# V loaded in three pieces between the pieces of w_in, the first FFN banks filled by head pairs, and a quarter of the first K loaded in float32 on another queue

## The chip, the cores and the metric

The kernel runs on one core of one Trainium2 chip. Times are device microseconds of that core. A "run" is one execution; a kernel's figure is the median of its runs. A profile is taken of one execution, and the spans and points in time in the text are that execution's. Engines: PE (TensorE matmul), PEld (its weight loads), DVE (VectorE), ACT (ScalarE), POOL (GpSimd), SP (SyncE).

## The reference

```
k_proj = einsum('ks,bhsd->bhkd', E, k)            # E, F: 64 x 1024
v_proj = einsum('ks,bhsd->bhkd', F, v)            # q, k, v: (8, 8, 1024, 64) float32
attn   = softmax(q @ k_proj^T / 8)
x      = (attn @ v_proj) as (8*1024, 512)
out    = relu(x @ w_in)^2 @ w_out                 # w_in 512 x 2048, w_out 2048 x 512
```

Eight batches, eight heads. Per batch the attention is small, and two FFN layers of 128x512 matmuls follow. The inputs are float32; the kernel computes in bfloat16 and lets GpSimd's DMA cast on the way in.

## The kernel before

The FFN of batch b runs on PE while the attention of the next batches is put between its steps. Only the first batch has nothing to hide behind: its loads, its attention and the weights come one after the other. The parts that matter here, with cuts marked:

```
    out_pool = ctx.enter_context(tc.tile_pool(name="outp", bufs=4))
    ...
    nc.sync.dma_start(e_f32[:], E[:])                      # SyncE's queue, no cast
    ...
    for g in range(2):                                     # GpSimd's queue, float32 -> bf16
        load(K0[:, half[g]], tokens(k, 0, h=half[g]))
        load(Q0[:, half[g], 0:4, :], tokens(q, 0, h=half[g], i=slice(0, 4)))
        ...                                                # F after the first Q
    for g in range(2):
        load(V0[:, half[g]], tokens(v, 0, h=half[g]))
    ...
    W_IN_PIECES = ((0, 2), (2, 4), (4, 8), (8, 12), (12, 16))
    ...                                                    # five pieces of w_in
    for j in range(WP):                                    # four pieces of w_out
        if j == WP - 1:
            load(Q0[:, :, 4:8, :], tokens(q, 0, i=slice(4, 8)))
        ...
    warm(8)                                                # matmuls on zeros
    ET = projection("ET", e_bf)
    ...                                                    # K, scores, V of both halves, values
    # FFN of the first batch, first layer: blocks fb = 0..15, four matmuls each over cb = 0..3;
    # then the second layer, w_out pieces 0..3 for two row tiles, step by step.
    # After step 21: transposes of the second half of Q.
```

A cb is a pair of heads: block fb can be begun with the pairs 0 and 1 only.

The softmax here doesn't subtract the row's maximum and nothing guards it: scores larger than these inputs give would overflow.

## Time and profile before

| | |
|---|---|
| median of 3 runs | 512.42 us (511.7 to 512.67) |
| profiled span | 510.0 us |
| PE busy | 497.0 us, 97% |
| first FFN matmul | 21.67 us |
| last w_out piece lands, PE goes on with it | 42.31, 42.35 us |

PE is full almost everywhere after 42 us. So a gain has to come from before. There the chain of waits (start, duration, what, in us) is a chain of loads:

```profile
7.67 14.18 DMA w_in_116<-in_moe_w_in_dram
21.86 0.28 issue
22.14 20.17 DMA w_out_131<-in_moe_w_out_dram
42.31 0.04 issue
42.35 1.04 PE ps_bank L364 x4
```

GpSimd issues the last piece of w_out (w_out_131) when the second piece of w_in has landed; it lands at 42.31, and PE uses it at once. PE's own timeline (start, duration, line, operation, tiles, shapes, count, and the idle time before it with its cause) shows the two places that the change aims at:

```profile
19.74 1.06 PE L204 MATMUL ps_bank<-V_sb,FT 128*64 128x256 bf16 x16 [1.44 <-DMA V_sb<-in_v_dram]
...
21.67 1.31 PE L358 MATMUL ps_bank<-xT,w_in_114 128*128 128x512 bf16 x5
...
25.57 3.62 PE L358 MATMUL ps_bank<-xT,w_in_118 128*128 128x512 bf16 x16
...
40.24 1.06 PE L231 MATMUL ps_bank<-ident,Q_sb 128*128 128x128 bf16 x16
...
42.35 1.02 PE L364 MATMUL ps_bank<-w_out_131,hsq 128*128 128x512 bf16 x4 [0.19 <-DMA w_out_131<-in_moe_w_out_dram]
```

PE is idle for 1.44 us before the second half of V, the FFN starts at 21.67, and its first four blocks are done when the next line starts, at 25.57. The windows view of the DMA engines in the first microseconds (window and length, then PE, PEld, DVE, ACT, POOL busy, then granted clock, DMA share, GB/s):

```profile
2.00:3.00 1.00, 1.00 (x4) 0.42 (x3) 0.00 (x0) 0.02 (x1) 1.00 (x3) 1.00 0.90 168
3.00:4.00 1.00, 1.00 (x4) 0.33 (x3) 0.00 (x0) 0.00 (x0) 0.95 (x4) 1.00 0.67 144
4.00:5.00 1.00, 0.79 (x2) 0.00 (x0) 0.64 (x1) 0.00 (x0) 1.00 (x2) 1.00 1.20 198
```

A share over 1 means that packets overlap. GB/s counts the bytes written: a cast load writes half of the float32 bytes that it reads. From 4 us to 42 us the share is about 1.2 to 1.4, with 180 to 205 GB/s written at first and 205 from 22 us on. Only the first two microseconds of transfer are not full.

### The profile page before, as it was taken

To read this page: it belongs to the slowest core of one execution; us is meant where nothing else is said; L and a number is where in the kernel's file an instruction comes from. 1 tells how busy PE (TensorE), PEld (TensorE's weight loads), DVE (VectorE), ACT (ScalarE), POOL (GpSimd) and SP (SyncE) were. 2 spreads that over 40 slices of the span, in tenths; PEclk is the share of its full clock that TensorE was granted. 3 is DMA by queue.
4 is the path that set the end of the run, shared out by engine and by line. 5 is a ranking of instruction groups with operands and counts; after the bars stand their busy time and mean duration, and the time that the engine had idled before them with its cause. 6 is when DMAs were issued, how large, how long until landed. Compare 5 with 4: busy or idle time off the path is not lost.

```text
span 510.0 us, 6889 instructions
## 1 busy us (share of the span) xinstructions
PE 497.0 (97%) x2710; PEld 222.8 (44%) x2761; DVE 216.7 (42%) x437; ACT 272.4 (53%) x411; POOL 32.0 (6%) x44
## 2 busy tenths in 40 slices
PE   8799999999999999999999999999999999999997
PEld 4344444444444444444444444444444444444444
DVE  2442766444434445235452345444443443522130
ACT  2564484664718556374645736366472755544351
POOL 7320100121000020001000000000000000000000
PEclk9999999999999999999999999999999999999999
DMA  9999999899996199104931060101102011010102
GB/s 156 204 205 222 226 207 202 132 220 207 195 217 125 56 185 201 65 0 126 181 78 42 17 160 1 62 22 42 53 1 82 1 41 42 31 54 21 63 0 82
DMA packets 67840, 53.92 MB, mean 106 GB/s; under 512 B 29152, under 2 KB 59616, under 8 KB 67808
## 3 DMA queue, kind: packets, MB, share of 16 engines
q0 software_dynamic: 30880, 29.49, 36.8%
q1 hardware_dynamic: 36928, 23.99, 17.5%
q8 instruction: 21, 0.34, 0.3%
q14 instruction: 11, 0.09, 0.1%
HBM read 59.24 MB, written 16.78 MB: 149 GB/s over the span
## 4 chain that ended last, share of the span: by engine, by line
PE 88%; DMA 7%; issue 2%; POOL 1%; ACT 1%; DVE 1%; POOLq 0%; ACTq 0%
PE ps_bank L364 41%; PE ps_bank L358 40%; DMA w_out_131<-in_moe_w_out_dram 4%; DMA w_in_116<-in_moe_w_in_dram 3%; PE ps_bank L185 2%; PE ps_att L256 1%; PE ps_att L290 1%; PE ps_att L312 1%; PE ps_bank L312 1%; DVE rs L300 0%; PE ps_bank L241 0%; DVE xT L341 0%; POOL K_sb L76 0%; POOL V_sb L76 0%; ACT expT L270 0%
## 5 line engine op out<-in xcount | busy, mean ns | idle before, releaser
L355 DVE TENSOR_TENSOR hsq<-h_relu 128x512 bf16<-128x512 bf16 x256 | 108.9, 426 | 192.9 <-ACT h_relu L354 192.0
L354 ACT ACTIVATE h_relu<-ps_bank 128x512 bf16<-128x512 f32 x256 | 151.7, 599 | 69.3 <-PE ps_bank L358 69.2
L364 PEld LDWEIGHTS <-hsq 128*128 128x128 bf16 x1040 | 99.5, 98 | 123.6 <-issue 9.3
L371 ACT COPY o_sb<-ps_bank 128x512 f32<-128x512 f32 (+1 forms) x65 | 37.6, 579 | 119.7 <-PE ps_bank L364 110.9
L364 PE MATMUL ps_bank<-w_out_124,hsq 128*128 128x512 bf16 (+1 forms) x257 | 65.6, 376 | 0.2
L364 PE MATMUL ps_bank<-w_out_131,hsq 128*128 128x512 bf16 (+1 forms) x251 | 64.1, 376 | 1.4 <-issue 1.1
L364 PE MATMUL ps_bank<-w_out_128,hsq 128*128 128x512 bf16 (+1 forms) x252 | 64.3, 376 | 1.1 <-issue 1.0
L364 PE MATMUL ps_bank<-w_out_126,hsq 128*128 128x512 bf16 (+1 forms) x249 | 64.2, 376 | 1.1 <-issue 0.8
L300 DVE COPY rs<-rs 32x1024 f32<-32x1024 f32 x60 | 41.3, 689 | 47.2 <-ACT rs L295 45.8
L358 PE MATMUL ps_bank<-xT,w_in_122 128*128 128x512 bf16 x255 | 58.9, 380 | 0.0
L358 PE MATMUL ps_bank<-xT,w_in_118 128*128 128x512 bf16 x250 | 57.7, 380 | 0.4
L358 PE MATMUL ps_bank<-xT,w_in_120 128*128 128x512 bf16 x247 | 57.4, 379 | 0.4
L270 ACT ACTIVATE expT<-ps_att 128x1024 bf16<-128x1024 f32 x32 | 31.8, 1024 | 18.1 <-PE ps_att L256 18.1
L358 PEld LDWEIGHTS <-w_in_120 128*128 128x128 bf16 x256 | 24.9, 98 | 30.4 <-issue 0.4
L358 PEld LDWEIGHTS <-w_in_118 128*128 128x128 bf16 x256 | 24.9, 98 | 30.2 <-issue 0.4
L358 PEld LDWEIGHTS <-w_in_122 128*128 128x128 bf16 x256 | 24.4, 98 | 31.1 <-issue 2.7
L358 PE MATMUL ps_bank<-xT,w_in_114 128*128 128x512 bf16 x128 | 30.6, 379 | 0.3 <-DVE xT L341 0.2
L358 PE MATMUL ps_bank<-xT,w_in_116 128*128 128x512 bf16 x126 | 30.0, 379 | 0.1
L294 ACT ACTIVATE rs<-ps_att 128x1024 f32<-128x1024 f32 x15 | 15.3, 1023 | 12.7 <-PE ps_att L290 12.7
L316 DVE TENSOR_TENSOR xT<-ps_att,rs 128x512 bf16<-128x512 f32 x28 | 18.1, 686 | 8.7 <-PE ps_att L312 8.4
L358 PEld LDWEIGHTS <-w_in_114 128*128 128x128 bf16 x128 | 12.4, 98 | 15.6 <-issue 1.3
L358 PEld LDWEIGHTS <-w_in_116 128*128 128x128 bf16 x128 | 12.5, 98 | 15.2 <-issue 0.2
(71 smaller groups left out, 233.9 us busy)
## 6 DMA issues: line engine op xcount, KB each, us to landing
out_dram<-o_sb SPq DMA_DIRECT2D x63, 256.0 KB, 2.0
K_sb<-in_k_dram POOLq DMA_DIRECT2D x7, 1024.0 KB, 22.1
V_sb<-in_v_dram POOLq DMA_DIRECT2D x7, 1024.0 KB, 26.7
Q_sb<-in_q_dram POOLq DMA_DIRECT2D x7, 1024.0 KB, 15.0
K_sb<-in_k_dram POOLq DMA_DIRECT2D x2, 512.0 KB, 7.1
V_sb<-in_v_dram POOLq DMA_DIRECT2D x2, 512.0 KB, 12.0
Q_sb<-in_q_dram POOLq DMA_DIRECT2D x2, 256.0 KB, 7.6
w_in_118<-in_moe_w_in_dram POOLq DMA_DIRECT2D x1, 512.0 KB, 15.5
```

The lines of the kernel that those rows point to most:

```text
L185: nc.tensor.matmul(ps[LO, :], lhsT=ET[:, i, :], rhs=self.K[:, :, i, :], start=f, stop=l)
L256: nc.tensor.matmul(ps[o, par], lhsT=self.kT[r, h % 4, h // 4, :], rhs=self.qT[r, h, n, :], start=True, stop=True)
L270: nc.scalar.activation(e[:], ps[:], AF.Exp, scale=SCALE)
L294: nc.scalar.activation(rs[1][:], ps[:], AF.Ln)
L300: nc.vector.tensor_copy(rs[j][lack:lack + 32], rs[j][have:have + 32])
L312: nc.tensor.matmul(ps_x[par][o], lhsT=self.vp[r, 2 * pr + a, :], rhs=e[r, par], start=True, stop=True)
L316: nc.vector.tensor_tensor(out=self.xT[:, pr, :, par], in0=ps_x[par].rearrange("p (c t) -> p c t", c=2), in1=rs[:, par].rearrange("p (c t) ...
L354: nc.scalar.activation(r[:], ps[:], AF.Relu)
L355: nc.vector.tensor_tensor(out=self.hsq[c][:, fb, :], in0=r[:], in1=r[:], op=ALU.mult)
L358: nc.tensor.matmul(ps[:], lhsT=w_in_blk(cb, fb), rhs=self.xT[:, cb, c].rearrange("p a t -> p (a t)"), start=(cb == 0), stop=(cb == NCB - 1),)
L364: nc.tensor.matmul(ps[:, m], lhsT=self.hsq[c][:, fb, tb * P:(tb + 1) * P], rhs=w_out_blk(fb)[:, m], start=(fb == 0), stop=(fb == NFB - 1),)
L371: nc.scalar.copy(o[:, m], ps[:, m])
```

## The change

Its intent: start the FFN before all of V is there, and load two heads of the first K without a cast, by a queue that starts earlier. The diff, cut:

```
+    k_f32 = soft_pool.tile([P, 2, NI, D], F32, tag="rs", name="k_f32")
+    nc.sync.dma_start(k_f32[:], tokens(k, 0, h=slice(0, 2)))
...
     for g in range(2):
-        load(K0[:, half[g]], tokens(k, 0, h=half[g]))
+        h = slice(2 if g == 0 else 4, 4 * g + 4)
+        load(K0[:, h], tokens(k, 0, h=h))
...
-    for g in range(2):
-        load(V0[:, half[g]], tokens(v, 0, h=half[g]))
+    V_PIECES = (slice(0, 4), slice(4, 6), slice(6, 8))
+    load(V0[:, V_PIECES[0]], tokens(v, 0, h=V_PIECES[0]))
...
     for j, (lo, hi) in enumerate(W_IN_PIECES):
         ...                                     # the piece of w_in
+        if j < 2:
+            load(V0[:, V_PIECES[j + 1]], tokens(v, 0, h=V_PIECES[j + 1]))
...
-                    banks = [bank() for _ in range(2)]
-                    for g in range(2):
-                        for fb in range(2):
-                            for cb in (2 * g, 2 * g + 1):
+                    banks = [bank() for _ in range(4)]
+                    for cbs, fbs in (
+                        ((0, 1), (0, 1)), ((0, 1), (2, 3)), ((2,), (0, 1)), ((2,), (2, 3)), ((3,), (0, 1, 2, 3)),
+                    ):
+                        for fb in fbs:
+                            for cb in cbs:
                                 self.first_mm(c, fb, cb, banks[fb])
...
+        nc.scalar.copy(K0[:, 0:2], k_f32[:])
...
-        att.project_v(1)
-        att.chunk_values(0, 1)
...
+                at(1, att.project_v, V_PIECES[1])
+                at(2, att.chunk_values, 0, 1, (0,))
+                at(2, att.project_v, V_PIECES[2])
+                at(3, att.chunk_values, 0, 1, (1,))
```

More of the change, by code (lines that the diff above doesn't have):

```diff
@@ L111 @@
     w_in_at, w_out_sb = {}, []
-    for lo, hi in W_IN_PIECES:
+    for j, (lo, hi) in enumerate(W_IN_PIECES):
         t = wpool.tile([P, NCB, (hi - lo) * P], BF16, name=f"w_in_{lo}")
@@ L197, in project_k, with project_v @@
             self.keep_k(ps[LO, 0:C // 2], g, nc.scalar.copy if g == 0 else None)
-        def project_v(self, g):
-            ps = bank()
+        def project_v(self, h):
+            n = (h.stop - h.start) * D
+            ps = att_psum()[:, 0, 0:n]
             for i in range(NI):
@@ L204, in project_v @@
                     nc.tensor.matmul(
-                        ps[o, 0:C // 2], lhsT=FT[:, i, :], rhs=V0[:, half[g], i, :],
-                        start=(i == 0), stop=(i == NI - 1),
+                        ps[o], lhsT=FT[:, i, :], rhs=V0[:, h, i, :], start=(i == 0), stop=(i == NI - 1)
                     )
-            nc.vector.tensor_copy(self.vp[:, half[g]], ps[:, 0:C // 2].rearrange("k (h d) -> k h d", d=D))
+            nc.vector.tensor_copy(self.vp[:, h], ps.rearrange("k (h d) -> k h d", d=D))
         def transpose_k(self, gs=(0, 1)):
@@ L331, in chunk_sums, with chunk_values @@
             self.rs[g] = self.inverse(ps)
-        def chunk_values(self, c, g):
+        def chunk_values(self, c, g, pairs=(0, 1)):
             ps = att_psum()
-            e, rs = self.e.pop(g), self.rs.pop(g)
-            for j in range(2):
+            e, rs = self.e[g], self.rs[g]
+            for j in pairs:
                 s = slice(j * HC, (j + 1) * HC)
                 self.values_mm(ps[:, :, s], 2 * g + j, e[:, :, s])
-            for j in range(2):
+            for j in pairs:
                 s = slice(j * HC, (j + 1) * HC)
@@ L380, in steps @@
                 if first:
-                    banks = [bank() for _ in range(2)]
-                    for g in range(2):
-                        for fb in range(2):
-                            for cb in (2 * g, 2 * g + 1):
+                    banks = [bank() for _ in range(4)]
[4 more added lines that the diff above has]
+                            for cb in cbs:
                                 self.first_mm(c, fb, cb, banks[fb])
-                            if g == 1:
+                            if cbs[-1] == NCB - 1:
                                 self.square(c, fb, banks[fb])
-                        yield
-                    fb0 = 2
+                        if (cbs, fbs) != ((2,), (2, 3)):
+                            yield
+                    fb0 = 4
                 for fb in range(fb0, NFB):
@@ L448 @@
         warm(2)
-        att.project_v(0)
+        att.project_v(V_PIECES[0])
         warm(1)
@@ L452 @@
         att.chunk_values(0, 0)
-        warm(1)
-        att.project_v(1)
-        att.chunk_values(0, 1)
+        warm(2)
         coming = None
```

## The prediction

> **What bounds the kernel now.** PE is busy 97% of the 510.0 us span (page, part 1) at a granted clock of 1.0, and the windows view shows it at 99% or so from 42.35 us on. The gain left lies before that. There PE works 17.06 of the first 21.67 us (with warm-up matmuls) and 20.17 of the next 20.68. In the chain of waits that stretch is DMA: w_in_116 (second w_in piece) lands at 21.86, GpSimd then issues the last w_out piece, which lands at 42.31, and PE, having waited only 0.19 us, goes on at 42.35. So PE and the load stream arrive together at 42.3 us. The DMA engines never rest before that: 205 GB/s (written bytes) in 21.67:42.35, one 512 KB piece per about 2.55 us, in order of issue.
>
> **What the change does.**
> 1. FFN start. Now the first FFN matmul waits for the second half of V (landed 19.7) and runs at 21.67. After the change w_in's first piece comes straight behind V's first half (16.0), so the first four FFN matmuls can run about 18.5 to 19.5. The price: V projection in 32 small matmuls among the FFN (about 1.3 us; L204's 16 of 256 columns take 1.06), and waits for V's last piece (about 21 to 21.5) and for two more rounds of copy, values, multiply. I expect the first four FFN blocks finished about 24.3 instead of 25.6: PE gains 1 to 1.5 us on the old order.
> 2. That alone gives nothing at 42.3: the bytes ahead of the last w_out piece are the same, so PE would just wait there about 1 us.
> 3. K in float32. 256 KB leave GpSimd's cast stream (1.28 us at 205 GB/s) and become 512 KB on SyncE's queue. The Trainium skill ("DMA: Bandwidth & Descriptors", section "Issuing engines are not separate DMA queues") says that all queues run on the same 16 engines, so this is no free bandwidth; in this trace the casts read about 410 GB/s of float32 and lone stores move 330 GB/s, so the 512 KB cost an estimated 1.3 to 1.55 us of the engines. What is won is that it fills the start: the first E packet runs at 2.1, the first cast packet at 3.2, and the engines are about half used from 2.5 to 4.0 (windows view: DMA share 0.90 and 0.67 against 1.2 to 1.4 later), an estimated 0.7 us of lost transfer time. Net: the cast stream, the last w_out piece too, lands about 0.6 us earlier (0.2 to 1.0). ScalarE's cast (about 1.0 us, as L270 of that size) fits before the ET copy ends at 6.37 and costs nothing.
>
> **On the critical path:** only the shift of the stream, about 0.6 us; after 42 us everything moves by it.
>
> **Prediction: 511.6 us, 80% range 510.4 to 512.6; faster by over 2% 0.01, within 2% 0.98, slower 0.01.**
>
> **What would show the steps.** Right: first FFN matmul before 19.5; the fourth FFN block done about 1.3 us earlier; last w_out piece landing at 41.3 to 42.1, and PE waiting 0.5 us or more for it (now 0.19); DMA share above 1 in 2:4. Wrong: w_out landing at 42.3 or later (the float32 load only pushes the casts back); PE idle over 2 us between 19 and 24.
>
> **What would make it wrong:** float32 loads that share the engines worse than estimated; E delayed by K; the new order of GpSimd's loads starving the stream; or something else in the stream relaxing, for 1.5 us or more.

## The result, and the profile after

The changed kernel took 512.45 us (median of 6 runs, 511.94 to 513.01), beside 512.54 us for before in the same rounds and its earlier runs. The ratio is 0.9993, with a 95% interval of 0.9975 to 1.001: the same. A ratio is the mean time of one kernel's runs over that of the other's of the same rounds, so not quite the ratio of the medians. The predicted 511.6 us lies 0.85 below; the range holds the result.

The chain of waits after:

```profile
8.37 13.37 DMA V_sb<-in_v_dram
21.74 0.28 issue
22.02 20.25 DMA w_out_134<-in_moe_w_out_dram
42.27 0.04 issue
42.31 1.04 PE ps_bank L370 x4
```

It is the same chain with other names, and it ends 0.04 us earlier, not 0.6. PE's timeline:

```profile
18.51 0.38 PE L364 MATMUL ps_bank<-xT,w_in_115 128*128 128x512 bf16 x1 [0.34 <-DVE xT L347]
...
21.78 0.64 PE L211 MATMUL ps_att<-V_sb,FT 128*64 128x128 bf16 x16
22.66 0.59 PE L364 MATMUL ps_bank<-xT,w_in_115 128*128 128x512 bf16 x2 [0.24 <-DVE xT L347]
...
24.28 0.59 PE L364 MATMUL ps_bank<-xT,w_in_115 128*128 128x512 bf16 x2 [0.26 <-DVE xT L347]
...
25.34 3.61 PE L364 MATMUL ps_bank<-xT,w_in_121 128*128 128x512 bf16 x16
...
42.31 1.02 PE L370 MATMUL ps_bank<-w_out_134,hsq 128*128 128x512 bf16 x4 [0.37 <-DMA w_out_134<-in_moe_w_out_dram]
```

The FFN starts 3.2 us earlier (18.51), but its first four blocks are done at 25.34, only 0.23 us before the old order. The last piece of V lands at 21.74, and from there the work goes through projection, copy, values and multiply, with PE waiting on DVE twice more (0.24 and 0.26 us). What PE gained, it then spends waiting for w_out. The windows view of the first transfers:

```profile
2.00:3.00 1.00, 1.00 (x4) 0.41 (x3) 0.00 (x0) 0.03 (x1) 1.00 (x4) 1.00 0.87 164
3.00:4.00 1.00, 1.00 (x4) 0.32 (x3) 0.00 (x0) 0.00 (x0) 0.93 (x4) 1.00 1.04 279
4.00:5.00 1.00, 0.79 (x2) 0.00 (x0) 0.60 (x1) 0.00 (x0) 1.00 (x2) 1.00 1.06 369
```

The float32 load fills 3 to 4 us (share 1.04 instead of 0.67), but it does nothing for 2 to 3 us. From 4 to 5 us, 369 GB/s instead of 198 is no gain: 198 GB/s of casts written are about 396 read. The first packet of GpSimd's casts runs at 4.84 us, where it ran at 3.22 before (from the packets of the trace). By 8 us the stream was about 0.4 us ahead all the same (by the packets, and counting the two heads of K as the 256 KB that they are in bfloat16, 874 KB against 791, at 205 GB/s). Then it slowed down: from 8 to 9 us the windows view shows 135 GB/s, where before has 196, and by 10 us about 0.15 us of the lead was left. Why it slowed down there is open.

One more thing. The profiled span of after is 1.2 us longer than before's, although its lead at 42 us is 0.04. I lined the two traces up at ScalarE's 65 copies of output tiles. After leads by 0.04 us from the first copy to the fourteenth (144 us) and is 1.34 us behind from the sixteenth (155 us) to the end. So the whole of it was lost between 144 and 155 us. The waits in 140:158 us (engine and line, what it waited for, us, times, longest), before:

```profile
ACT o_sb L371 <- DMA out_dram<-o_sb: 7.5, 2, 5.5
```

and after:

```profile
ACT o_sb L377 <- DMA out_dram<-o_sb: 8.9, 2, 7.7
...
PE ps_bank L364 <- ACT o_sb L377: 1.1, 2, 0.8
```

ScalarE's copy waits for an output buffer, because four stores are stuck on SyncE's queue: a DMA transpose of Q was issued there at 116.09 and holds the queue until 138.61, and the first store behind it was issued at 138.71 and landed at 152.26 (before: 137.38 and 150.13). In before the wait ends just in time, and its view has no line in which PE waits for the copy; here PE has to wait for its bank.

### The profile page after: what moved, and what is told of

Its sections match the earlier page's. It is cut to its first block, busy times and chain, and to the rows that moved or that the text cites. A ratio compares the mean times of both kernels' runs of the same rounds, so it can differ in the third digit from the quotient of the medians.

```text
span 511.2 us, 6930 instructions
## 1 busy us (share of the span) xinstructions
PE 498.3 (97%) x2727; PEld 223.3 (44%) x2778; DVE 217.0 (42%) x438; ACT 273.2 (53%) x412; POOL 33.0 (6%) x45
## 4 chain that ended last, share of the span: by engine, by line
PE 85%; DMA 9%; issue 2%; ACT 2%; POOL 1%; DVE 1%; SPq 0%; POOLq 0%; ACTq 0%
PE ps_bank L364 40%; PE ps_bank L370 38%; DMA w_out_134<-in_moe_w_out_dram 4%; DMA V_sb<-in_v_dram 3%; PE ps_bank L191 2%; DMA out_dram<-o_sb 2%; PE ps_att L262 1%; PE ps_att L296 1%; PE ps_att L318 1%; PE ps_bank L318 1%; DVE rs L306 1%; ACT rs L301 0%; ACT rs L300 0%; PE ps_bank L247 0%; ACT expT L276 0%
```

## The experiments

Theories: **G** (gate): PE and the load stream meet at the last w_out piece; its landing decides. Rival **P**: PE's order in the first blocks decides. **S** against **N**: the late stores take away, or do not take away, what the start gains. Later **C**: PE's clock at the start matters for the new order.

For every trace I read three times. "Landed" is when the last w_out piece has landed. "PE ready" is when PE could have started on that piece: its weight load for that matmul plus 0.21 us, the distance of the two where nothing held the matmul back. "Lag" is the end of the first and of the seventeenth output copy against before's (43.99 and 171.01 us); the difference of the two lags is what was lost in between, mostly at the late stores. "Full clock from" is the start of the trace's first record of the full granted clock.

| run | full clock from | PE ready | landed | lag, copy 1 | lag, copy 17 |
|---|---|---|---|---|---|
| before | 5.3 | 41.99 | 42.31 | 0 | 0 |
| after | 5.6 | 41.77 | 42.27 | -0.04 | 1.34 |
| e1_again | 4.2 | 41.57 | 41.73 | -0.57 | 0.26 |
| e2_no_f32 | 4.6 | 41.84 | 42.51 | 0.21 | 0.41 |
| e3_f32_only | 9.7 | 41.59 | 41.93 | -0.37 | 1.29 |
| e4_v_two | 9.5 | 42.51 | 41.95 | 0.18 | 0.12 |
| e5_before_b8 | 4.7 | 41.51 | 42.02 | -0.29 | -0.35 |
| e6_after_b8 | 9.3 | 42.96 | 41.87 | 0.62 | 0.56 |
| e7_v_two_b8 | 9.4 | 42.34 | 42.28 | 0.01 | -0.05 |
| e8_q_late | 4.1, half rate again 7.5 to 10.9 | 41.85 | 39.64 | -0.48 | 0.70 |
| e9_after_b8_warm | 4.7 | 41.53 | 42.07 | -0.23 | -0.29 |
| e10_before_b8_cold | 12.6 | 43.00 | 42.64 | 0.66 | 0.60 |
| e11_after_b8_cold | 10.5 | 43.31 | 42.09 | 0.97 | 0.91 |
| e12_q_late_warm | 4.3 | 40.50 | 39.29 | -1.84 | -0.65 |

(Copy 1 of e8 and e12 stands elsewhere in the order of work, so only their copy 17 compares. Their "PE ready" does not compare either: 16 transposes of Q, about 0.9 us of PE, stand before the last w_out piece in the other kernels and behind it in these two.) All twelve kernels gave the correct result. Four kernels at a time shared a chip and the runs of before.

### e1_again: the changed kernel once more

No edit.

> The changed kernel, unchanged, for a second trace and a tighter ratio. Theory G (gate): PE meets the load stream at the last w_out piece, so that piece's landing decides the time; it landed at 42.27 against 42.31 before, so the ratio is 0.999 to 1.001 and the landing again within 0.15 us of 42.3. Theory N (noise): the 1.38 us that the profiled run lost at 144 to 155 us, behind a late DMA transpose on SyncE's queue and late stores, is chance and comes in some runs of both kernels; then this trace shows another loss there, anything from 0 to 1.5 us. If it belongs to the change, it is there again with 1.1 to 1.5 us of PE idle.

Measured: 512.4 us, ratio 0.9996 (0.998 to 1.0012), before 512.68. The ratio is as theory G has it, but the landing is not: 41.73 us, 0.58 before the old one and 0.54 before the same kernel's first trace. So the stream varies by half a microsecond between runs of one kernel, and this trace shows the shift that I had predicted. The loss at the late stores was there again, but 0.83 us instead of 1.38. Expected for chance was anything from 0 to 1.5; it is neither absent nor of one size, so this trace alone does not tell chance from the change (see e5 and e6).

### e2_no_f32: without the float32 K

```
-    k_f32 = ...; nc.sync.dma_start(k_f32[:], ...)
-        h = slice(2 if g == 0 else 4, 4 * g + 4)
+        h = half[g]
-        nc.scalar.copy(K0[:, 0:2], k_f32[:])
```

> The change without the float32 K: V in three pieces and the FFN by head pairs stay. Theory G: first FFN matmul near 18.9 (0.35 later than after), last w_out piece lands at 42.5 to 42.6 (before's 42.31 plus about 0.2 for the extra piece), time 0.1 to 0.3 us over before, ratio 1.000 to 1.001. Rival P (PE's early start is worth something by itself): time 0.2 us or more below before although the stream is not earlier.

Measured: 512.34 us, ratio 0.9998 (0.9984 to 1.0011). First FFN matmul at 18.69, landing at 42.51, as theory G had it; PE was ready 0.67 us before. Theory G holds in the trace: the FFN starts 3 us earlier, and the first output copy ends 0.21 us later than before.

### e3_f32_only: before, with only the float32 K

```
+    k_f32 = ...; nc.sync.dma_start(k_f32[:], tokens(k, 0, h=slice(0, 2)))
+        h = slice(2 if g == 0 else 4, 4 * g + 4)
+        load(K0[:, h], tokens(k, 0, h=h))
+        nc.scalar.copy(K0[:, 0:2], k_f32[:])
```

> Before, with two heads of K in float32 through SyncE's queue and nothing else. Theory G with the stream earlier by 0.35 us (what the loads of K and Q showed in after): last w_out piece lands at 41.9 to 42.1, PE arrives for it at the same time as before or 0.3 earlier, span 0.2 to 0.35 us below before, ratio 0.9993 to 0.9996. My prediction's term (0.6 us won at the start): landing at 41.6 to 41.8. First cast packet at 4.8, not 3.2, in either case.

Measured: 512.04 us, ratio 0.9989 (0.9973 to 1.0005). Landing at 41.93, first output copy 0.37 us earlier: with the float32 K alone the stream is 0.38 us earlier than in before, and PE follows it. One trace does not show that the float32 K made this shift: e5, the old order without it, landed at 42.02. It then lost 1.66 us at the late stores, so its profiled span was 511.2. One expectation failed: the first cast packet ran at 3.54, not 4.8 (4.20 in e1_again). The casts do not simply queue behind the float32 load; how the engines share the two queues differs from run to run.

This trace also showed something that I had not looked for: PE ran at half rate from 5.9 to 9.7 us (see e6), and yet PE was ready at 41.59. In the old order the wait for V hides a slow start.

### e4_v_two: V's second half in one piece

```
-    V_PIECES = (slice(0, 4), slice(4, 6), slice(6, 8))
+    V_PIECES = (slice(0, 4), slice(4, 8))
-        if j < 2:
+        if j < 1:
-                at(2, att.chunk_values, 0, 1, (0,))
-                at(2, att.project_v, V_PIECES[2])
-                at(3, att.chunk_values, 0, 1, (1,))
+                at(1, att.chunk_values, 0, 1)
```

> After, with V's second half in one piece behind w_in's first piece, so the chain from V to the last xT is one round of copy, values and multiply instead of two. PE should finish the first four FFN blocks at 24.0 to 24.5 instead of 25.3. Theory G: that buys nothing, PE waits 1.0 us or more for the last w_out piece (0.37 in after), which lands at 42.1 to 42.3, and the time is that of after within 0.2 us. Rival P: the time falls by 0.8 us or more with the earlier blocks.

Measured: 511.9 us, ratio 0.9988 (0.9975 to 1.0002), 0.5 us in the median below e1_again of the same rounds, between what G and P expected. The trace cannot tell them apart, because PE started slowly in it (half rate up to 9.5 us), the blocks were done about 26 us, and PE came after the landing. So PE was not waiting for the stream here at all, and the 0.5 us are inside the noise of the runs.

### e5_before_b8 and e6_after_b8: the late stores taken away

Both with this edit, nothing else; a copy then finds a free buffer while four stores wait:

```
-    out_pool = ctx.enter_context(tc.tile_pool(name="outp", bufs=4))
+    out_pool = ctx.enter_context(tc.tile_pool(name="outp", bufs=8))
```

> Before with eight output buffers instead of four, to take away the wait that ScalarE's output copy has near 145 to 152 us for a store that stands behind a DMA transpose on SyncE's queue. Theory S (the late stores take away what the start gains, and are the spread of the runs): no PE idle at 144 to 156 us, runs spread by less than 1 us (before: 511.5 to 514.3), median 0.3 to 1.0 us below before. Rival N (the spread comes from elsewhere, the start or the launch): spread and median as before.

> After with eight output buffers. Theory S: PE loses nothing at 144 to 156 us, and what is left against the same change of before is the lead at the last w_out piece alone: 0.05 to 0.6 us below e5_before_b8, ratio to before 0.997 to 0.999. Rival N: the median stays within 0.2 us of after's 512.4.

Measured: e5 511.63 us (511.36 to 512.54), e6 511.97 us (511.07 to 512.4), before in the same rounds 512.42 (511.44 to 515.23). Both ratios are 0.9981 (0.9954 to 1.0007 and 0.9957 to 1.0006). In both traces the lag no longer changes between copies 1 and 17, within 0.06 us: the loss is gone, as theory S has it. The six runs each of e5 and e6 spread by 1.2 and 1.3 us, the eleven of before by 3.8. The gain of the median is inside the intervals, so S is shown in the traces and only likely in the times. Two expectations failed: e5's spread was to be under 1 us, and e6 was to be 0.05 to 0.6 us below e5, but its median is 0.34 above.

The record speaks against the late stores being the change's doing. The first store behind the transpose lands at any time from 150.13 to 152.37 us in the fourteen traces, and in the old order too (151.50 in e5, 151.73 in e10); before's 150.13 is the earliest of all. In the six traces with four buffers the loss grows with this landing, taken less the trace's own lag at copy 1: 150.13 in before and 150.46 in e4, with no loss; 151.17, 151.79, 152.30 and 152.74 in e2, e1, after and e3, with 0.20, 0.83, 1.38 and 1.66 us. So before's trace was a lucky one, and much of after's extra 1.2 us of span comes from comparing with it. A lead at the start makes the copies come sooner, and these stores do not follow.

With the stores out of the way the change is still worth nothing: 0.9981 against 0.9981. And e6's trace is 0.62 us behind before at copy 1, although its stream landed at 41.87. The reason is at the start. PE's timeline of after:

```profile
5.82 1.04 PE L151 MATMUL ps_bank<-zeros 128*128 128x512 bf16 x4
6.84 1.03 PE L200 MATMUL ps_bank<-K_sb,ET 128*64 128x256 bf16 x8
```

and of e6:

```profile
5.90 1.89 PE L151 MATMUL ps_bank<-zeros 128*128 128x512 bf16 x4
7.72 1.82 PE L200 MATMUL ps_bank<-K_sb,ET 128*64 128x256 bf16 x8
```

The same matmuls take 1.89 and 1.82 us instead of 1.04 and 1.03: half rate, until 9.3 us. The windows view prints a granted clock of 1.00 for these stretches too; durations tell it. The Trainium skill ("TensorE: Matmul & The Clock Gate", section "What's actually happening") says that the clock doubles after a busy window of about 3.4 us, and that this window is free-running, so that the moment varies from run to run. The traces agree: in e7, PE does the same as in after up to 5.8 us, and gets the full clock at 9.4 instead of 5.6; and in e8 the clock records change at 4.12, 7.53 and 10.95 us, 3.4 us apart.

For the old order such a start is free (e3: PE ready at 41.59). For the new order it is not (e6: 42.96, 1.2 us later than after's 41.77), because the idle 1.44 us before the second half of V, in which it could be made up, is what the change has removed.

### e7_v_two_b8: V in two pieces, eight buffers

The edits of e4 and e5 together.

> V's second half in one piece, with eight output buffers. Theory G (the landing of the last w_out piece decides): PE has the first four FFN blocks done at 24.0 to 24.6 when PE's clock is full at the start, waits 0.7 to 1.5 us for the last w_out piece at about 42, and the time is that of e6_after_b8 within 0.2 us. Rival P (PE's order decides): 0.6 us or more below e6_after_b8.

Measured: 511.46 us (511.21 to 512.05), ratio 0.9974 (0.995 to 0.9998), 0.5 us below e6 in the median, as e4 was below e1. The premise failed again: PE started slowly, so it was ready at 42.34 and met the landing at 42.28. Against e6, also slow at the start, it was ready 0.6 us sooner. So in these two traces the order with one round of copy, values and multiply does count when PE comes late, as rival P says; the difference of the times is inside the noise. I cannot tell how many of the timed runs start slowly, since they have no trace.

### e8_q_late: the gate moved

```
-        if j == WP - 1:
-            load(Q0[:, :, 4:8, :], tokens(q, 0, i=slice(4, 8)))
+    load(Q0[:, :, 4:8, :], tokens(q, 0, i=slice(4, 8)))       # after the last w_out piece
-                at(21, ...transpose_q_chunk x2)  at(23, ...chunk_scores x2)  at(25, att.sums, 0)
-                at(27, ...chunk_values x2)
+                at(25, ...transpose_q_chunk x2)  at(26, ...chunk_scores x2)
+                at(28, att.chunk_sums, 1, 0)  at(29, att.chunk_sums, 1, 1)
+                at(31, att.chunk_values, 1, 0)  at(32, att.chunk_values, 1, 1)
-                if first:                                     # banks by head pairs
+                if self.cold:                                 # ... in the second chunk as well
```

> e7 with the gate moved: the second half of Q is loaded after the last w_out piece, 512 KB less ahead of it, so that it lands at 39.3 to 39.8 instead of 42; the attention of the second chunk starts three steps later, with one sum per head group, and its FFN is filled by head pairs too. Theory G: now the early FFN start counts; the first output copy comes 1.0 to 1.6 us earlier than in e7, and the time is 0.7 to 1.5 us below e7's, if the later chunk does not stall PE by more than 0.5 us at 50 to 53 us. Rival P: no gain over e7, or a loss.

Measured: 511.0 us (510.73 to 512.31), ratio 0.9971 (0.9945 to 0.9996). The piece landed at 39.64, as expected, and PE passed it without a wait. But the profiled run (512.31, its slowest) was again one with half rate at the start, from 7.5 to 10.9 us, so PE was the late one: it began the piece 0.5 us before the old order did, but with about 0.9 us of transposes still to do, and was 0.70 behind at copy 17. The median is 0.46 below e7's, by the ratios only 0.15 us: less than theory G wanted, and no proof against P.

### e9_after_b8_warm, e10_before_b8_cold, e11_after_b8_cold: PE's clock at the start

```
-        warm(8)
+        warm(10)          # e9;  e10 and e11: warm(2)
```

e9 and e11 are e6 with that edit, e10 is e5 with it.

> After with eight output buffers and ten instead of eight warm-up matmuls at the start, which fill PE's idle 0.4 to 0.6 us before the transposes of E. Theory C (PE's clock at the start is a matter of chance in the runs: half rate up to 9.3 to 9.7 us in five of the seven float32 runs, full from 4.2 to 5.6 in the others; full rate is worth something to the new order): full rate from 7.5 us or sooner, the projection of K in about 1.05 us and not 1.9, last FFN block of the first four begun before 24.5, median 0.2 to 0.6 us below e6_after_b8. Rival N (the clock at the start is hidden behind the loads): half rate or not, the median is that of e6_after_b8 within 0.15 us.

> Before with eight output buffers and two warm-up matmuls instead of eight, so PE runs at half rate until about 9 us or later in every run. Theory C: the wait for V's second half (1.28 to 1.44 us of PE idle) hides most of it: median 0 to 0.4 us over e5_before_b8. Rival: it is in the time in full, 1.4 us over e5_before_b8.

> After with eight output buffers and two warm-up matmuls instead of eight. Theory C: the new order has used up the idle time in which before hides a slow start, so PE comes late to the last w_out piece, the first FFN matmul is at 19.8 or later, and the median is 0.8 to 1.5 us over e9_after_b8_warm, and 0.4 to 1.2 over e10_before_b8_cold. Rival N: within 0.2 us of e9_after_b8_warm and of e10_before_b8_cold.

Measured: e9 511.56 us (511.18 to 512.87), ratio 0.9982 (0.9969 to 0.9996). e10 511.43 us (511.18 to 512.29), ratio 0.9979 (0.9966 to 0.9993). e11 512.51 us (511.77 to 512.72), ratio 0.9993 (0.9978 to 1.0007).

e9 had the full clock from 4.7 us. It was 0.41 below e6 in the median, but the ratio to before is that of e6 (0.9982 against 0.9981), so what two more warm-up matmuls bring is not shown. Its trace is the cleanest picture of the gate. PE's timeline of e9:

```profile
42.11 1.02 PE L370 MATMUL ps_bank<-w_out,hsq 128*128 128x512 bf16 x4 [0.42 <-DMA w_out<-in_moe_w_out_dram]
```

and of e5, the old order, also with the full clock:

```profile
42.06 1.02 PE L364 MATMUL ps_bank<-w_out,hsq 128*128 128x512 bf16 x4 [0.38 <-DMA w_out<-in_moe_w_out_dram]
```

Old order or new, PE stands at the same piece, and goes on at the same time.

With two warm-up matmuls both traces start at half rate (the timed runs have no trace). e11 takes 1.1 us more than e10 in the median (0.7 by the ratios, 0.9993 over 0.9979; the means of the runs of these rounds differ by 0.75, with a 95% interval of about 0.1 to 1.4), and 0.95 more than e9, while e10 is no slower than e5 by the ratios. That is theory C: in the times, a cold start costs the new order more than the old one. The direction is shown, the size is not. Nor is it free for the old order in every case. In the two traces the difference is only 0.3 us at copy 1: e10's profiled run was its slowest, with full clock from 12.6 us only and the stream late (its first K landed at 8.33 us, in e5 at 6.85). The second half of V was there at 19.41, but PE came to it at 20.73, and was ready for the w_out piece at 43.00, 1.5 us after e5. So in these traces the old order hides a slow start as far as its idle time before V reaches, and no further.

### e12_q_late_warm: a version that beats before

e8 with `warm(10)`.

> The candidate for a version that beats both: V in two pieces, eight output buffers, the second half of Q behind the last w_out piece, and ten warm-up matmuls. Theory G and C together: last w_out piece at 39.3 to 39.8, PE there at 40.3 to 40.9 without waiting, median 510.0 to 510.7, against 511.0 of e8_q_late, which had a slow start in its profile. If the later chunk eats the gain, the median is 510.9 or more and PE waits show at 50 to 54 us.

Measured: 510.95 us (510.63 to 511.06), before 512.73 in the same rounds, ratio 0.9965 (0.9953 to 0.9978): 0.35% faster, small but clear of the noise. (After was not run in these rounds; its ratios of 0.9993 and 0.9996 lie above this interval. Eight buffers alone gave 0.9981 in e5, so about half of the gain may be theirs. Of the same rounds, all five runs of e12 lie below all six of e9, which has the eight buffers and the warm start too.) The last w_out piece landed at 39.29, and PE, with the full clock from 4.3 us, runs through it without a gap. PE's timeline of e12:

```profile
35.33 7.93 PE L369 MATMUL ps_bank<-w_out,hsq 128*128 128x512 bf16 x35
43.09 1.06 PE L236 MATMUL ps_bank<-ident,Q_sb 128*128 128x128 bf16 x16
```

PE was ready at 40.50, 1.5 us before PE in the old order, which then had to wait on top: it began the piece 1.84 us later. But about 0.9 us of that is the 16 transposes of Q, which the old order has behind it by then (40.24 to 41.14) and e12 does after the piece (43.09). At copy 17 the lead is 0.65. The waits view shows no wait of PE for another engine over 0.4 us from 40 us on, so what is given back is mostly this work in another order and not a new wait. The median missed the expected 510.0 to 510.7 by 0.25. e12 bundles four edits; that the moved gate is the one that makes the early FFN count is what e9 (waits) and e12 (does not) suggest together in their traces. They differ in V's pieces too, and no run separates the two with a full clock.

## Why the prediction was right or wrong

- **The result** was predicted as within 2%, 511.6 us, and is 512.45, inside the range. The predicted gain of about 0.8 us on before is not there. The range also holds before's own 512.42, so that the result lies in it says nothing for the mechanism: a change without any effect would have done as well.
- **What bounds the start** was right. PE meets the load stream at the last w_out piece; an early FFN alone gains nothing (e2: FFN 3 us earlier, first output copy 0.21 us later).
- **"I expect the first four FFN blocks finished about 24.3 instead of 25.6"** was wrong: 25.34. The last piece of V landed at 21.74, beyond the predicted 21 to 21.5, and the two rounds of copy, values and multiply behind it were named as a price but given no size; PE waited for DVE's multiplies before four groups of matmuls (0.34, 0.22, 0.24 and 0.26 us). PE's gain at the w_out piece was 0.22 us (ready at 41.77 instead of 41.99), not 1 to 1.5.
- **"Net: the cast stream, the last w_out piece too, lands about 0.6 us earlier (0.2 to 1.0)"** had too large a size, and its mechanism is likely but not shown. It was 0.04 in the first trace and 0.58 in the second of the same kernel. Over the traces with the old place of Q, the landing is 42.02 on average with the float32 K (eight traces, 41.73 to 42.28) and 42.37 without (four, 42.02 to 42.64): about 0.35 us, while the traces of either kind spread by 0.55 and 0.62. The estimate that an idle 0.7 us would be filled was half right: nothing more ran in 2 to 3 us, where the share was 0.87 after 0.90. And the idle time from 3 to 4 us is not in every run of a kernel without the float32 K: the share there is 0.67 in before, 0.84 in e2 and 0.99 in e5.
- **The Trainium skill ("DMA: Bandwidth & Descriptors", section "Issuing engines are not separate DMA queues")** says that the queues run on the same engines. The traces agree: in after the casts' first packet came 1.62 us later, and 256 KB less of them are worth 1.28 us at 205 GB/s (an estimate); what can be won is only what the engines had idle.
- **"After 42 us everything moves by it"** failed as well. PE has to wait once more, at 144 to 155 us, by way of a DMA transpose, late stores and four output buffers. There the traces lost 1.38 us (after), 0.83 (e1), 0.20 (e2), 1.66 (e3) and next to nothing (before, e4), while the lead that the start brought was at most 0.57. How much is lost is mostly a matter of when the first of these stores lands, in the old order as in the new one. In the six traces with eight buffers whose copies compare, the lag changes by 0.06 us at most.
- **Not foreseen:** the half-rate start. It is hidden in the old order as far as its idle time before V reaches (e3 does not pay, e10's trace does) and costs the new one about 1.2 us at the w_out piece (e6 against after). In the traces with eight warm-up matmuls it came in five of seven with the float32 K (e8 in part) and in none of three without. Whether the float32 load makes it likelier, by way of E landing later (4.34 to 4.98 us), is open: after and e7 have the same PE timeline up to 5.8 us and differ.
- **Open:** in what share of the timed runs the start is slow. So I do not claim how the zero of the result is made up of a small gain at the gate, a loss in slow starts, and the late stores; only that each is seen in traces, and that without the late stores the change is still worth nothing (e5 and e6).

## What to carry to other kernels

Where compute and a load stream meet at the same point, making one of them earlier is worth only the distance to the other; measure both arrival times at the meeting point before shortening either, and move the meeting point (here by loading half of Q later) if you want an early start to count. An idle gap can be a buffer against run-to-run variation, and taking it out makes the kernel pay for a slow clock that it did not feel before. When the expected gain is below a microsecond, line the traces up at repeated events: the whole difference may come from one late store 100 us further on, and not from the change.

## What the Trainium skill lacked or had wrong

- "TensorE: Matmul & The Clock Gate", section "Why this matters for your kernels", warns of PE-idle gaps over about 3 us. Here a shorter gap went with the loss of the full clock: in e8 it came at 4.12 us, PE was idle for 1.42 us and then did eight transposes, and from 7.53 to 10.95 us it was at half rate again. In after and e7 the same gap of 0.41 us and the same transposes were followed by the full clock at 5.6 us in one and at 9.4 in the other, so the gap alone does not decide. The page does say, in its section "Part 4: PE-mode transpose", that transposes do not count as busy in the same way; how much of it is theirs, no run shows.
- "DMA: Bandwidth & Descriptors" gives no rate for loads that cast. Here the stream from float32 to bfloat16 wrote 205 GB/s, so it read about 410 GB/s of float32; in the plain float32 load's fastest microsecond the view shows 369 GB/s, a few casts among them.
- The same page, section "Queues, rings and completion order", describes turns between the queues packet by packet. Here the first cast packet ran at 3.20 to 3.49 us in the four traces without a float32 load of K on the other queue, and at anything from 3.54 to 4.96 us in the ten with it; the page does not lead one to expect either the size or the spread.
- No page tells what a DMA transpose costs those behind it on its queue: SyncE was held for 22.5 us at 116 us in after (by the next such transpose, at 178 us, for 4.1), and the store behind it took 13.55 us from issue to landing, where the median store takes 2.0.
